# The 64-row stores of an output stage: two issuing queues, or one

## The chip, the cores and the metric

One core of one Trainium2 chip. The metric is device time in microseconds (us) of one execution; medians of several executions are quoted, and lower is better. The program runs for some 437 us; the change touches only its last 25.

## The reference, cut to what matters

Attention with a forget gate over 8 batches of 576 rows, then a mixing of the 64 lowest Fourier modes over the sequence, and a last step that adds, multiplies and clips:

```python
    X = np.fft.rfft(x, axis=1)                        # x: attention output (8, 576, 512)
    ...                                               # 64 modes times w_r, w_i
    y = np.fft.irfft(Y, n=S, axis=1)
    u = x + y
    return (u + np.maximum(u @ w_ch, 0.0)).astype(np.float32)     # (8, 576, 512), 9.44 MB
```

The kernel makes `u` and `z = u @ w_ch` as sums in PSUM, and the last line above is its output stage.

## The kernel before

Two batches form a pair. A pair's 576 rows are four blocks of 128 and a last one of 64; the two last blocks share one tile, batch b in partitions 0 to 63 and batch b+1 in partitions 64 to 127. Each "job" is one such tile. For each job PE fills `pu` and `pz`, Activation copies `pu` to SBUF (`emit_u`), VectorE adds the clipped `pz` (`emit_o`), and the result is stored. Jobs are pipelined by one: the copy for the next job is issued ahead of the sum for this one.

```python
        def emit_u(job, ps, u, split=False):
            ...
                nc.scalar.copy(u[:, bs, :], ps[0][:, bs, :])

        def emit_o(job, ps, u, o, pair, split=False):
            ...
                nc.vector.scalar_tensor_tensor(
                    o[:, bs, :], ps[1][:, bs, :], 0.0, u[:, bs, :], ALU.max, ALU.add
                )
                ...
                if sb == 4:                                   # the 64-row job of a pair
                    for h in range(2):
                        eng = (nc.sync, nc.scalar)[h]
                        eng.dma_start(
                            out[b + h, 512:576, :], o[64 * h : 64 * h + 64, 0, :]
                        )
                ...
                elif sb % 2 or n_wide < 2:                    # wide jobs: 512 KB a batch
                    ...
                        nc.sync.dma_start(...)
...
            if not last:
                uo_n = outs(jobs[n + 1])
                emit_u(jobs[n + 1], nxt, uo_n[0])
            emit_o(job, ps, *uo, n == 0)
```

There are four pairs; "the very last" half-store is the fourth pair's. In profile lines the tile of a 64-row job is `uo` (as is that of the first pair's other jobs), that of wide jobs `us` and `os`. An engine's sequencer is the part of it that issues instructions and transfers; what has been issued on a queue and not yet moved I call its ring. A **half-store** below is one of the eight stores of 64 rows, 128 KB in packets of 2,048 bytes.

The softmax here doesn't subtract the row's maximum and nothing guards it: scores larger than these inputs give would overflow.

Of the kernel before, what the change touches and what calls it, by code (L numbers as in the profile page):

```python
# [21 lines left out]
def kernel(  # L22
# [11 lines left out]
    nc = tc.nc  # L34
# [194 lines left out]
    with ExitStack() as actx:  # L229
# [486 lines left out]
        for s in range(NS + 1):  # L716
            pr, h = s // 2, s % 2
# [37 lines left out]
    with ExitStack() as bctx:  # L755
# [216 lines left out]
        def wide(job):  # L972
            return len(job) == 2 and job[0][0] != job[1][0]
# [28 lines left out]
        def emit_o(job, ps, u, o, pair, split=False):  # L1002
            for i in range(2 if split else 1):
                bs = slice(i, i + 1) if split else slice(0, len(job))
                nc.vector.scalar_tensor_tensor(  # L1005
                    o[:, bs, :], ps[1][:, bs, :], 0.0, u[:, bs, :], ALU.max, ALU.add
                )
                b, sb = job[0]
                n_wide = 4 * (b // 2 - 1) + sb
                if sb == 4:  # L1010
                    for h in range(2):
                        eng = (nc.sync, nc.scalar)[h]
                        eng.dma_start(
                            out[b + h, 512:576, :], o[64 * h : 64 * h + 64, 0, :]
                        )
                elif not wide(job):
                    nc.sync.dma_start(
                        out[b, 128 * sb : 128 * sb + 256, :].rearrange(
                            "(p r) e -> p r e", r=2
                        )[:, bs, :],  # L1020
                        o[:, bs, :],
                    )
                elif sb % 2 or n_wide < 2:
                    rs = slice(sb % 2 if n_wide < 2 else 0, sb % 2 + 1)
                    for j, (bj, _) in enumerate(job):
                        nc.sync.dma_start(
                            out[bj, 128 * (sb - sb % 2) :, :][0:256, :].rearrange(
                                "(p r) e -> p r e", r=2
                            )[:, rs, :],
                            pair[:, j, rs, :],  # L1030
                        )
# [12 lines left out]
        jobs = []  # L1044
# [42 lines left out]
        for n, job in enumerate(jobs):  # L1087
            last = n == len(jobs) - 1
            zs = terms(job, ps, 1, "xy" if n else "y")
            us = []  # L1090
            if not last:
                nxt = start(n + 1)
                us = terms(jobs[n + 1], nxt, 0, "xy")
            if n == 0:
                run(us)
                run(zs)
            elif n == 1:
                run(terms(job, ps, 1, "x"), terms(jobs[2], nxt, 0, "x"))
                run(terms(job, ps, 1, "y"))
                run(terms(jobs[2], nxt, 0, "y"))  # L1100
            elif wide(job):
                run(zs)
                run(us)
            elif len(job) == 1:
                run(us)
                run(zs)
            else:
                run(zs, us)
# [5 lines that stand above are left out]
                ps, uo = nxt, uo_n  # L1114
# [28 lines left out]
```

## Time and profile before

| | |
|---|---|
| time, median (lowest to highest) | 437.63 us (437.6 to 438.23), 3 runs |
| span of the profiled execution | 436.5 us |
| first 64-row job starts on VectorE | 410.29 us |
| last VectorE result / last store landed | 428.16 / 435.40 us |
| half-stores on Sync / on Activation | 4 / 4 |

I call the time from the first 64-row job's start on VectorE to the last landing "the stage". It has two parts: **feed**, to the last VectorE result (428.16 - 410.29 = 17.87 us), and **drain**, from there to the last landing (7.24 us). The lines of the chain, the timelines and the DMA rate are in the prediction.

### The profile page before, as it was taken

The page shows a single profiled execution, that of the slowest core. Times are in us where ns is not written, and L with a number is a line of the kernel's source. Part 1 is how long each engine was busy: PE and PEld are TensorE (multiplying, and loading weights), DVE is VectorE, ACT ScalarE, POOL GpSimd, SP SyncE. Part 2 cuts the span into 40 slices and gives each one's busy share as a digit, 9 for nine tenths or more (in the row PEclk, how much of TensorE's full clock was granted, in tenths as well). Part 3 has the DMA queues.
Part 4 walks back from the last instruction along what each step waited for, and adds up shares of the span by engine and source line. Part 5 has one row for each costly group of instructions (what it writes and reads, how often), then busy time and mean ns, then how long its engine had stood idle before and what let it go on. Part 6 is the DMA issues. An engine that isn't in the chain of part 4 may idle for free.

```text
span 436.5 us, 12293 instructions
## 1 busy us (share of the span) xinstructions
PE 357.7 (82%) x5295; PEld 243.4 (56%) x5313; DVE 263.8 (60%) x658; ACT 224.7 (51%) x340; POOL 128.9 (30%) x202
## 2 busy tenths in 40 slices
PE   3787798999797886877877886999979978899881
PEld 2454666776675665565655665766644544454440
DVE  5797888877565564665666677333233645553892
ACT  2887489775444636436447282233424434542670
POOL 7333332423233233232332232332223232200500
PEclk9996899998766857758759597799999999989997
DMA  8999999999999999999999999999999999994797
GB/s 175 236 235 237 239 235 238 235 211 237 233 215 237 226 223 237 211 237 234 214 237 211 211 212 211 211 211 212 211 212 211 211 211 211 211 211 84 273 341 276
DMA packets 50981, 97.37 MB, mean 223 GB/s; under 512 B 3792, under 2 KB 12976, under 8 KB 50928
## 3 DMA queue, kind: packets, MB, share of 16 engines
q0 software_dynamic: 46688, 86.16, 100.7%
q1 hardware_dynamic: 3920, 9.91, 6.3%
q8 instruction: 41, 0.67, 0.6%
q10 hardware_dynamic: 320, 0.52, 0.5%
q14 instruction: 12, 0.10, 0.1%
HBM read 163.73 MB, written 9.44 MB: 397 GB/s over the span
## 4 chain that ended last, share of the span: by engine, by line
DMA 40%; PE 26%; ACT 10%; DVE 7%; issue 4%; POOL 0%; DVEq 0%; ACTq 0%
DMA wb<-in_moe_w_i_dram 39%; ACT E L576 7%; PE pav L614 6%; PE ps L569 5%; PE A L188 5%; PE tp L307 4%; ACT KT L320 2%; DVE QTs L322 2%; PE vp L541 2%; DVE os L1005 1%; PE px L657 1%; PE pz L828 1%; ACT VT L326 1%; PE px L682 1%; DVE E L591 1%
## 5 line engine op out<-in xcount | busy, mean ns | idle before, releaser
L576 ACT ACTIVATE E<-ps 128x1024 bf16<-128x1024 f32 (+1 forms) x128 | 101.4, 851 | 21.7 <-PE ps L569 11.3
L188 PE MATMUL A<-XT,wb 128*128 128x16 bf16 x1984 | 70.4, 181 | 13.6 <-DMA wb<-in_moe_w_i_dram 8.9
L188 PEld LDWEIGHTS <-wb 128*128 128x128 bf16 x1984 | 63.7, 99 | 27.3 <-issue 11.4
L93 POOL DMA_DIRECT2D wb<-in_moe_w_r_dram x64 | 42.4, 663 | 119.6 <-DMA wb<-in_moe_w_r_dram 21.9
L569 PE MATMUL ps<-QTs,KT 64*128 64x64 bf16 (+4 forms) x384 | 56.8, 316 | 19.6 <-ACT E L576 17.7
L93 POOL DMA_DIRECT2D wb<-in_moe_w_i_dram x64 | 42.3, 661 | 87.3 <-DMA wb<-in_moe_w_i_dram 43.9
L614 PE MATMUL pav<-va,E 128*128 128x65 bf16 (+1 forms) x1088 | 53.1, 205 | 3.2 <-DVE x_all L636 2.6
L614 PEld LDWEIGHTS <-E 128*128 128x128 bf16 (+1 forms) x1088 | 43.5, 111 | 18.4 <-issue 9.3
L591 DVE TENSOR_TENSOR E<-E,trimask 128x256 bf16<-128x256 bf16 (+2 forms) x128 | 36.9, 302 | 20.5 <-ACT E L576 20.2
L867 ACT CAST XW<-pxw 128x512 bf16<-128x512 f32 x36 | 20.8, 587 | 39.4 <-PE pxw L860 34.5
L326 ACT COPY VT<-tp 128x640 bf16<-128x640 bf16 (+1 forms) x32 | 23.2, 761 | 32.4 <-PE tp L307 32.4
L569 PEld LDWEIGHTS <-KT 64*128 64x128 bf16 x384 | 18.8, 97 | 32.5 <-issue 20.9
L860 PE MATMUL pxw<-wch,yy 128*128 128x512 bf16 x133 | 35.1, 398 | 1.3 <-issue 0.5
L910 ACT CAST XW<-pB 128x512 bf16<-128x512 f32 x36 | 21.0, 586 | 27.8 <-PE pB L828 27.7
L320 ACT COPY KT<-tp 128x640 bf16<-128x640 bf16 (+1 forms) x32 | 21.9, 748 | 25.9 <-PE tp L307 25.8
L909 DVE CAST x_all<-pA 128x512 bf16<-128x512 f32 x36 | 24.9, 692 | 14.0 <-PE pA L828 12.4
L322 DVE COPY QTs<-tp 128x640 bf16<-128x640 bf16 (+1 forms) x32 | 23.4, 767 | 14.3 <-PE tp L307 14.0
L636 DVE TENSOR_TENSOR x_all<-pav,rcp 128x384 bf16<-128x384 f32 x64 | 29.1, 455 | 0.9
L153 DVE TENSOR_TENSOR YTe<-A,Yacc 128x128 bf16<-128x128 f32 x16 | 5.9, 367 | 33.1 <-PE A L188 33.1
L828 PEld LDWEIGHTS <-ident_bf 64*64 64x64 bf16 (+1 forms) x348 | 15.8, 108 | 17.9 <-issue 8.9
L625 DVE RECIPROCAL rcp<-pav 128x6 f32<-128x6 f32 x64 | 12.1, 189 | 20.0 <-PE pav L614 19.4
L860 PEld LDWEIGHTS <-yy 128*128 128x128 bf16 x144 | 12.7, 101 | 15.2 <-DVE yy L854 4.6
(143 smaller groups left out, 622.2 us busy)
## 6 DMA issues: line engine op xcount, KB each, us to landing
wb<-in_moe_w_r_dram POOLq DMA_DIRECT2D x62, 512.0 KB, 16.9
wb<-in_moe_w_i_dram POOLq DMA_DIRECT2D x62, 512.0 KB, 17.8
stv<-in_v_dram POOLq DMA_DIRECT2D x10, 576.0 KB, 15.1
out_dram<-os SPq DMA_DIRECT2D x10, 512.0 KB, 5.0
stk<-in_k_dram POOLq DMA_DIRECT2D x11, 288.0 KB, 15.3
stq<-in_q_dram POOLq DMA_DIRECT2D x11, 288.0 KB, 15.3
wx<-in_v_dram POOLq DMA_DIRECT2D x5, 576.0 KB, 15.5
out_dram<-uo SPq DMA_DIRECT2D x3, 512.0 KB, 4.0
```

Source lines behind the costliest of these rows:

```text
L93: keep(nc.gpsimd.dma_start(dst, src))
L188: ins = nc.tensor.matmul(A[:, eb, mi, :], lhsT=w_of(mi, eb * 128), rhs=x_of(m), start=(i == 0), stop=(i == len(terms) - 1),)
L320: nc.scalar.copy(rows(KTs[pr % 2][:, :, 0:S]), tv)
L322: ins = nc.vector.tensor_copy(rows(QT[pr][:, :, :]), tv)
L326: nc.scalar.copy(rows(VTs[pr % 2][:, :, 0:S]), tv)
L569: nc.tensor.matmul(ps[:, b, o : o + n], lhsT=KTs[pr % 2][bs, h, jb * 128 : (jb + 1) * 128], rhs=QT[pr][bs, h, jb * 128 + c0 : jb * 128 + c ...
L576: nc.scalar.activation(E[:, :, piece * 512 : piece * 512 + w], ps[:, :, 0:w], ACT.Exp, scale=scale,)
L591: nc.vector.tensor_tensor(dg, dg, tr, ALU.mult)
L614: nc.tensor.matmul(pav[64 * half : 64 * half + w, slot, :], lhsT=E[:, b, c : c + (w - 1) * st + 1 : st], rhs=va[:, jb, b, :], start=(n == ...
L636: nc.vector.tensor_tensor(xo, pi, ri, ALU.mult)
L860: nc.tensor.matmul(pxw[:, :], lhsT=xT[:, eb, i * 128 : (i + 1) * 128], rhs=wch[:, eb, :], start=(eb == 0), stop=(eb == NDC - 1),)
L909: nc.vector.tensor_copy(xs, pA[:, :])
```

## The change

Its intent: stop the Activation engine from issuing stores between its copies. Only the very last half-store, when Activation has nothing else left, stays on its queue.

```diff
-                        eng = (nc.sync, nc.scalar)[h]
+                        eng = nc.scalar if job is jobs[-1] and h else nc.sync
```

## The prediction

> **What bounds the kernel now.** I read the slices of the page first, then the DMA queues and issues, then the last 30 us in three views: the chain that ended last, the timelines of the Activation and Sync engines, and the DMA's rate in stretches of that time. The changed line runs only there.
>
> The slices (10.9 us each) show a kernel that reads weights at the DMA's pace until about 400 us; the last three slices are the output stage, with the DMA engines 70 to 90% busy and 273 to 341 GB/s moved.
>
> ```profile
> DMA  8999999999999999999999999999999999994797
> GB/s 175 236 235 237 239 235 238 235 211 237 233 215 237 226 223 237 211 237 234 214 237 211 211 212 211 211 211 212 211 212 211 211 211 211 211 211 84 273 341 276
> ```
>
> The issues (KB each, median us to landing) say how much the change touches: eight stores of 128 KB, four on each queue. Three of the four on the Activation queue move to the Sync queue, 0.39 MB of 9.44 MB written.
>
> ```profile
> out_dram<-uo SPq DMA_DIRECT2D x4, 128.0 KB, 5.6
> out_dram<-uo ACTq DMA_DIRECT2D x4, 128.0 KB, 5.2
> ```
>
> The chain of the output stage (start us, us, what) shows where an Activation issue is on the path. "ACTq L1013" is the store's issue on the Activation sequencer; here it stands between one VectorE result and the next Activation copy.
>
> ```profile
> 410.29 0.70 DVE uo L1005
> 411.00 0.02 issue
> 411.02 0.57 ACTq L1013
> 411.59 0.04 issue
> 411.63 1.02 ACT us L1000
> 412.65 0.02 issue
> 412.67 1.23 DVE os L1005
> ```
>
> It occurs once. In the second and third pair the timeline of the Activation engine has the issue in time that the engine spends waiting for PE anyway: the copy at 417.33 follows the end of the `pu` matmuls at 417.31 (chain: 416.84 + 0.47), while the issue had ended at 416.79 + 0.49 = 417.28.
>
> ```profile
> 415.58 1.02 ACT L1000 COPY us<-pu 128x1024 f32<-128x1024 f32 x1
> 416.79 0.49 ACTq L1013 DMA_DIRECT2D out_dram<-uo  x1
> 417.33 3.02 ACT L1000 COPY us<-pu 128x1024 f32<-128x1024 f32 x3 [0.73 <-PE pu L828]
> ```
>
> The DMA rate in stretches (columns: stretch, us, busy time of PE, PEld, DVE, ACT and POOL with counts, granted clock, DMA share, GB/s) is the view that decides the end:
>
> ```profile
> 416.50:417.00 0.50, 0.50 (x16) 0.35 (x12) 0.32 (x2) 0.09 (x1) 0.00 (x0) 1.00 0.10 37
> 417.00:418.50 1.50, 1.42 (x32) 0.75 (x25) 1.29 (x2) 1.17 (x2) 0.00 (x0) 1.00 1.03 401
> 418.50:421.00 2.50, 2.12 (x38) 1.28 (x32) 2.50 (x3) 1.96 (x3) 0.00 (x0) 1.00 0.97 290
> 421.00:424.00 3.00, 2.45 (x44) 1.29 (x40) 2.69 (x3) 2.28 (x4) 0.00 (x0) 1.00 1.02 411
> 424.00:426.00 2.00, 1.63 (x26) 0.84 (x28) 1.93 (x2) 1.92 (x3) 0.00 (x0) 1.00 1.00 304
> 428.00:430.00 2.00, 0.00 (x0) 0.00 (x0) 0.16 (x1) 0.00 (x0) 0.00 (x0) 1.00 1.04 420
> 430.00:434.70 4.70, 0.00 (x0) 0.00 (x0) 0.00 (x0) 0.00 (x0) 0.00 (x0) 0.71 0.79 274
> ```
>
> The DMA runs dry once, at 416.5 (37 GB/s), and from 417 to 430 its engines are about 100% busy. The last compute instruction ends at 428.16 (VectorE, 427.48 + 0.68), the last packet about 434.7, the last landing is 435.4, the span 436.5: the end is a backlog of stores. Supply and drain are nearly equal: VectorE makes a pair's 4 x 512 KB + 2 x 128 KB = 2.36 MB in 5.70 us (`uo` starts at 416.08, 421.78, 427.48), 414 GB/s; the DMA drains at 401 to 420. Yet in two stretches it moves only 290 and 304 GB/s while as busy. By the packet records these are the times when packets of the Activation queue are in flight: its 64 packets of 2,048 bytes are spread from 418.5 to 421 and from 424 to 426. There they took a mean of 134 to 222 ns per half microsecond, and the Sync queue's 4,096-byte packets 183 to 217; with the Sync queue alone the same sizes took 84 and 160 ns.
>
> **What the Trainium skill says.** "DMA: Bandwidth & Descriptors", section "Issuing engines are not separate DMA queues": stores from Sync and Activation end on the same 16 engines and interleave, and a second issuer saves only sequencer time. The trace agrees that one queue fills the engines (420 GB/s at share 1.04 with the Sync queue alone). Section "Queues, rings and completion order" of that page: an engine takes the rows that have work in turn, a packet at a time. The trace agrees as far as the 64 Activation packets lie scattered among Sync packets over 2 us. That such turns lower the rate no page states; I have it from the packet times alone. "Perfetto Trace Analysis", section "DMA Instruction — HWDGE (DVE, Sync)": an issue's span is waiting for the descriptor generator and generating, not the movement. So long Sync issues (0.53, 0.76, 1.42 and 1.76 us for the four 128 KB stores, though all are alike) are back-pressure of a full ring; the Activation issues stay at 0.47 to 0.57.
>
> **The change, part by part.** The order of instructions on PE, VectorE and POOL is the same in both kernels; Activation loses three issues, Sync gains three, each right behind its twin.
>
> (1) Removed from Activation: 3 issues of 0.57, 0.49 and 0.47, 1.53 us. On the path only the first. Without it the copy at 411.63 can start when its `pu` matmuls end, about 411.07 (the last two start at 410.50 and take 0.55); it ends at 412.10, and VectorE, which finishes its previous `os` at 412.12, goes on at 412.15 instead of 412.67. That is 0.52 us, and all later work of the stage, whose VectorE gaps are 0.2 us, moves with it; the rows of `yy` it needs have landed by 414.1, before use. The second and third give 0.03 each: 0.05 us at most.
>
> (2) Added to Sync: 3 issues. In the first pair 0.4 to 0.55 us behind 411.54, done by 412.1 when the next `os` is ready. In the second, 417.3 to about 418.1, while Sync waits until 419.1. In the third Sync would be held from about 424.1 to 425.5, with the next `os` ready at 424.8 (425.33 less 0.52): 0.7 us late. But such an issue is long because the ring is full, so the engines have work: nothing on the path.
>
> (3) DMA rate. The hole at 416.5 moves 0.5 us earlier with its store. From then on, if mixing queues is what slows the two stretches, they go at about 405 GB/s: 2.5 us x 290 = 725 KB in 1.79 us, 0.71 saved; 2.0 x 304 = 608 KB in 1.50, 0.50 saved; 1.21 in all. I count a bit over half, 0.65: the first stretch is partly a ring running empty (share 0.97, not 1.03; the next `os` comes only at 419.6), and engines that finish at different times lose rate without any mixing. The tail from 430, where the very last 128 KB still goes on Activation, keeps its 274 GB/s.
>
> Sum: 0.5 + 0.65 = 1.15 us of 437.63: 436.5.
>
> **The rivals.** (a) Only the shift counts, the slow stretches are drain and imbalance: 437.1. For it: half of a pair's 128 KB was on Sync already, and 426.5 to 427.5 is at 334 GB/s with hardly any Activation packet. (b) The whole mixing loss comes back: 435.9. For it: the packet times double just there. (c) The end is set by drain alone and the time saved ahead only lengthens the backlog; nothing changes: 437.6. Against it: the DMA ran dry at 416.5, so it has been fed late. (d) The longer Sync sequence starves the engines or delays the last `os` by the 0.7 us of part 2: 438.2. Against it: the Sync ring holds over 2 us of work when its issues take 1.4 us (issued by 431.2, drained at 434.7). (e) The compute order shifts and a buffer wait appears; the nearest reuse, a buffer stored at 417.1 (landed 422.6) and rewritten at 425.2, leaves 2.6 us.
>
> **Range and chances.** From all of the mixing loss and a little more (435.4) to nothing or the loss of (d) cut short (437.7). Two per cent is 8.75 us, over a quarter of the whole output stage; no mechanism here comes near it, so within 2% has 0.98.
>
> **What would show it.** Right: no Activation issue between 410 and 413, the second `os` of the first pair at about 412.15 rather than 412.67 (relative to the `uo` before it: 1.86 us after its start instead of 2.38); the last `uo` of VectorE 0.5 us earlier; and no stretch near 290 GB/s before the tail. If the rate in the stretches stays near 300 with one queue, the mixing step is wrong and (a) holds. If the hole at 416.5 closes or a new one opens between 419 and 426, parts 2 or 3 are wrong. If runs scatter by over 0.6 us, as the three of before do (437.6 to 438.23), the size can't be read from the medians alone.

## More of the kernel before

The wide stores have 128 partitions and most of them 512 KB in packets of 4,096 bytes.

One more answer of the rate view, for the hole and the drain (columns: stretch, us, busy time of PE, PEld, DVE, ACT and POOL with counts, granted clock, DMA share, GB/s):

```profile
416.00:417.00 1.00, 0.79 (x16) 0.57 (x19) 0.81 (x3) 0.59 (x1) 0.00 (x0) 1.00 0.43 162
...
428.16:435.40 7.24, 0.00 (x0) 0.00 (x0) 0.00 (x0) 0.00 (x0) 0.00 (x0) 0.76 0.78 286
```

In the first line the DMA has half run dry (share 0.43, 162 GB/s) while PE and VectorE work. In the last all engines are done, and 286 GB/s x 7.24 us = 2.07 MB of stores are still to move.

## The result, and the profile after

A ratio here is the mean time of one kernel's fast runs over that of the other's fast runs of the same rounds, so not quite the ratio of the medians that are quoted.

| | before | after | ratio (95% interval) |
|---|---|---|---|
| first rounds (6 and 6 runs) | 438.31 | 436.92 | 0.9968 (0.9953 to 0.9982) |
| repeated later (11 and 6 runs) | 438.10 | 437.80 | 0.9987 (0.9966 to 1.0009) |

The prediction was 436.5 us, 435.4 to 437.7, from a median of 437.63 for before. The first rounds fall inside it, and both ratios are within 2%. The repeat shows how thin the ground is: its median lies just outside the range, and its interval includes no change at all. Over both, the 12 runs of after have a mean of 437.20 us and the 17 of before 438.13, 0.93 us apart (0.84 if the 17 further runs of before are counted in, 438.03 over all 34); single runs of after scatter from 435.96 to 438.93. The repeat ran on another chip than the four experiments that came before it, so times are compared within the same rounds only.

The DMA's last three slices now carry 225, 374 and 293 GB/s; before they were 273, 341 and 276. The queues are as intended, seven half-stores on Sync and one on Activation:

```profile
out_dram<-uo SPq DMA_DIRECT2D x7, 128.0 KB, 4.7
out_dram<-uo ACTq DMA_DIRECT2D x1, 128.0 KB, 4.8
```

In the chain of the first pair, the Activation issue and the Activation copy are gone; the second `os` starts 0.01 us after PE's matmuls.

```profile
410.81 0.43 PE pu L828 x8
411.24 0.61 PE pz L828 x8
411.85 0.47 PE pu L828 x6
412.32 0.01 issue
412.33 1.24 DVE os L1005
```

And VectorE runs its four `os` without a gap, where before it idled 0.56 us ahead of the second:

```profile
411.09 4.73 DVE L1005 SCALAR_TENSOR_TENSOR os<-pz,us 128x1024 f32<-128x1024 f32 x4
```

The first `uo` now starts at 410.48, so that second `os` comes 1.85 us after it, where it was 412.67 - 410.29 = 2.38. The Activation timeline shows the reason: three copies in a row start at 411.29, 0.81 us after the `uo`, not 1.34 as in the kernel before.

```profile
411.29 3.20 ACT L1000 COPY us<-pu 128x1024 f32<-128x1024 f32 x3 [0.25 <-PE pu L828]
```

The Sync timeline (start, us for all the issues merged in a row, count) shows the other side: two half-stores hold the Sync sequencer 1.62 us in the first pair and 2.74 and 2.46 us in the next ones.

```profile
411.20 1.62 SPq L1013 DMA_DIRECT2D out_dram<-uo  x2
412.92 3.79 SPq L1026 DMA_DIRECT2D out_dram<-os  x6
416.80 2.74 SPq L1013 DMA_DIRECT2D out_dram<-uo  x2
419.63 3.25 SPq L1026 DMA_DIRECT2D out_dram<-os  x4
422.97 2.46 SPq L1013 DMA_DIRECT2D out_dram<-uo  x2
```

And the DMA rate, with the columns as above:

```profile
416.00:417.00 1.00, 1.00 (x24) 0.64 (x23) 0.81 (x2) 0.23 (x2) 0.00 (x0) 1.00 1.06 397
417.50:419.50 2.00, 1.54 (x28) 0.67 (x23) 1.79 (x3) 1.92 (x3) 0.00 (x0) 1.00 1.00 387
419.50:421.00 1.50, 1.50 (x24) 0.93 (x17) 1.50 (x2) 1.10 (x3) 0.00 (x0) 1.00 0.84 260
424.00:425.50 1.50, 1.12 (x22) 0.55 (x17) 1.50 (x2) 1.42 (x2) 0.00 (x0) 1.00 1.03 415
425.50:426.50 1.00, 0.92 (x12) 0.23 (x5) 1.00 (x2) 0.59 (x2) 0.00 (x0) 1.00 1.00 311
427.83:434.20 6.37, 0.00 (x0) 0.00 (x0) 0.00 (x0) 0.00 (x0) 0.00 (x0) 0.64 0.86 314
```

Three things are to be seen. The hole at 416.5 is closed: 397 GB/s, where the same microsecond of before had 162. There are still slow stretches, 260 and 311 GB/s, with Sync alone; in the first the engines are only 84% busy, so it also ran partly empty. And the drain is 6.37 us at 314 GB/s. Feed and drain by the two traces of each kernel:

| trace | feed | drain | stage |
|---|---|---|---|
| before, first / second | 17.87 / 17.88 | 7.24 / 7.45 | 25.11 / 25.33 |
| after, first / second | 17.35 / 17.42 | 6.37 / 6.67 | 23.72 / 24.09 |

So by the means of the traces the stage is 1.3 us shorter, 0.5 in the feed and 0.8 in the drain. The stage is a better measure than the run time, since what comes before it has nothing to do with the change and its end moves by 1.7 us from trace to trace (the first `uo` starts between 409.56 and 411.28 us in the nine traces).

### The profile page after: what moved, and what is told of

Same layout as the page of the kernel before. It is cut to its first block, busy times and chain, and to the rows that moved or that the text cites. A ratio compares the mean times of both kernels' runs of the same rounds, so it can differ in the third digit from the quotient of the medians.

```text
span 435.5 us, 12294 instructions
## 1 busy us (share of the span) xinstructions
PE 361.2 (83%) x5295; PEld 245.6 (56%) x5313; DVE 264.0 (61%) x658; ACT 224.8 (52%) x340; POOL 128.6 (30%) x202
## 3 DMA queue, kind: packets, MB, share of 16 engines
HBM read 163.73 MB, written 9.44 MB: 398 GB/s over the span
## 4 chain that ended last, share of the span: by engine, by line
PE 39%; DMA 23%; ACT 12%; DVE 10%; issue 4%; POOL 0%; DVEq 0%; ACTq 0%
DMA wb<-in_moe_w_i_dram 22%; ACT E L576 8%; PE pav L614 8%; PE A L188 7%; PE ps L569 7%; PE tp L307 5%; PE px L657 3%; DVE QTs L322 2%; PE vp L541 2%; PE pu L828 2%; ACT KT L320 2%; PE pz L828 1%; DVE XT L671 1%; DVE os L1005 1%; DVE E L591 1%
## 5 line engine op out<-in xcount | busy, mean ns | idle before, releaser
L569 PE MATMUL ps<-QTs,KT 64*128 64x64 bf16 (+4 forms) x384 | 58.2, 322 | 19.9 <-ACT E L576 17.9
L614 PE MATMUL pav<-va,E 128*128 128x65 bf16 (+1 forms) x1088 | 55.2, 209 | 3.1 <-DVE x_all L636 2.6
L614 PEld LDWEIGHTS <-E 128*128 128x128 bf16 (+1 forms) x1088 | 45.3, 114 | 18.7 <-issue 9.1
L867 ACT CAST XW<-pxw 128x512 bf16<-128x512 f32 x36 | 20.7, 586 | 35.7 <-PE pxw L860 23.5
L860 PE MATMUL pxw<-wch,yy 128*128 128x512 bf16 x133 | 33.6, 385 | 1.2 <-issue 0.7
L541 PE MATMUL vp<-ident_bf,VT 128*128 128x128 bf16 x160 | 17.1, 247 | 5.2 <-DVE QTs L322 4.6
```

The source lines that it names most:

```text
L541: nc.tensor.transpose(vp[:, sc, :, :].rearrange("p b d -> p (b d)"), VTs[s // 2 % 2][:, h, sc * 128 : (sc + 1) * 128], ident_bf[:, :],)
L569: nc.tensor.matmul(ps[:, b, o : o + n], lhsT=KTs[pr % 2][bs, h, jb * 128 : (jb + 1) * 128], rhs=QT[pr][bs, h, jb * 128 + c0 : jb * 128 + c ...
L614: nc.tensor.matmul(pav[64 * half : 64 * half + w, slot, :], lhsT=E[:, b, c : c + (w - 1) * st + 1 : st], rhs=va[:, jb, b, :], start=(n == ...
L860: nc.tensor.matmul(pxw[:, :], lhsT=xT[:, eb, i * 128 : (i + 1) * 128], rhs=wch[:, eb, :], start=(eb == 0), stop=(eb == NDC - 1),)
```

## The experiments

My theory: a path part (an Activation issue on the chain, 0.5 us) and a rate part (stores from two queues slow the DMA engines). Rivals: only the path; only the rate; and, for the rate, that half-stores are slow by themselves on whatever queue. All kernels up to the stores-only ones gave correct results. Their ratios are against the kernel before in the same rounds.

| run | ratio (95% interval) | feed | drain | stage |
|---|---|---|---|---|
| first pair only | 0.9979 (0.9965 to 0.9993) | 17.39 | 7.47 | 24.86 |
| first pair only, again | 0.9986 (0.9967 to 1.0005) | 17.40 | 6.59 | 24.00 |
| later pairs only | 0.9987 (0.9971 to 1.0002) | 17.86 | 6.82 | 24.69 |
| Activation issues deferred | 0.9995 (0.9977 to 1.0014) | 17.34 | 7.59 | 24.92 |
| all on Sync | 0.9977 (0.9964 to 0.9991) | 17.34 | 6.18 | 23.52 |
| before, again | 0.9999 (0.9983 to 1.0014) | 17.88 | 7.45 | 25.33 |

**First pair only.** The theory's path part by itself:

```diff
-                        eng = (nc.sync, nc.scalar)[h]
+                        eng = (nc.sync, nc.scalar)[h if b else 0]
```

> Only the first pair's second half-store goes to the Sync queue; those of the second and third pair stay on Activation. Theory (a path part and a rate part): VectorE's output stage, from the start of the first pair's uo to its last result, falls from 17.87 us to about 17.35, as in the changed kernel; the rate stays low while Activation packets fly in pairs two and three, so the end is only about 0.5 to 0.7 us earlier than before. Rival 'only the path': the whole 1.4 us of the changed kernel is here too (ratio 0.997). Rival 'only the rate': nothing is gained (ratio 1.000).

The feed is the changed kernel's, as every theory had it. The drain line:

```profile
426.96:434.43 7.47, 0.00 (x0) 0.00 (x0) 0.00 (x0) 0.00 (x0) 0.00 (x0) 0.64 0.77 284
```

It drains like the kernel before: 284 GB/s and 7.47 us. Of the 0.48 us gained in the feed 0.23 are given back in a longer drain. The hole at 416.5 closed here too (391 GB/s in the 1.3 us after the second `uo`). The time, 0.21% less or 0.9 us, lies between the theory's 0.5 to 0.7 and the whole 1.4, and its interval excludes neither.

**First pair only, once more**, because one trace decides little:

> First pair alone once more. If the shift of 0.52 us is mostly swallowed by the backlog of stores: stage 17.39 us and then about 7.4 us again, total 24.8, ratio 0.998 to 0.999. If it is handed on to the end: stage total 24.6 or less, with a drain of 7.2 us or less.

```profile
428.44:435.03 6.59, 0.00 (x0) 0.00 (x0) 0.00 (x0) 0.00 (x0) 0.00 (x0) 0.61 0.85 318
```

The same kernel, the same feed (17.40), and a drain 0.88 us shorter, at 318 GB/s. A single drain is therefore no proof of anything. Here the stage is 1.1 us shorter than in the first trace of before, so the shift is handed on and more. Whether it is or not changes from run to run.

**Later pairs only**, the complement:

```diff
-                        eng = (nc.sync, nc.scalar)[h]
+                        eng = nc.scalar if job[0][0] in (0, 6) and h else nc.sync
```

> The complement: the first pair's second half-store stays on Activation, those of pairs two and three go to Sync. Theory: VectorE's stage stays at 17.87 us; from its last result to the last landing 7.24 us falls to about 6.4, the end is 0.7 to 0.9 us earlier (ratio 0.998). Rival 'only the path': no gain (1.000). Rival 'only the rate': all 1.4 us (0.997).

```profile
427.90:434.72 6.82, 0.00 (x0) 0.00 (x0) 0.00 (x0) 0.00 (x0) 0.00 (x0) 0.56 0.87 314
```

No shift in the feed (17.86), and the drain is at 314 GB/s and 6.82 us: a stage 0.42 us shorter than in the first trace of before. The hole stays (216 GB/s in 415.82 to 417.12). The theory had the drain at about 6.4 us, so it gave half of what was expected. That speaks against "only the path" but doesn't rule it out: 0.42 us is less than the 0.88 by which the two drains of the first-pair kernel differ, and the ratio, 0.9987, is by itself not clear of 1.

**Deferred.** All queues as before, but the Activation issue is pinned three jobs later, behind the fourth `us` copy, where Activation idles:

```diff
-                        eng = (nc.sync, nc.scalar)[h]
-                        eng.dma_start(out[b + h, 512:576, :], o[64 * h : 64 * h + 64, 0, :])
+                        args = (out[b + h, 512:576, :], o[64 * h : 64 * h + 64, 0, :])
+                        if h == 0:
+                            nc.sync.dma_start(*args)
+                        elif job is jobs[-1]:
+                            nc.scalar.dma_start(*args)
+                        else:
+                            pending.append([3, args])
...                                                  # after emit_u of the next job
+                for x in pending:
+                    x[0] -= 1
+                while pending and pending[0][0] == 0:
+                    keep(nc.scalar.dma_start(*pending.pop(0)[1]))
```

> All queues as in the kernel before, but the Activation issue of each pair comes three jobs later, behind the fourth us copy, where Activation has 0.4 to 0.6 us idle. So the hold on the path is gone and the mixing of queues is not. Theory: VectorE's stage 17.35 to 17.45 us, end 0.5 us earlier than before, with rates of 290 to 340 GB/s while the Activation packets fly. Rival 'only the path': 1.4 us earlier, as the changed kernel. Rival 'mixing is all': no gain.

```profile
428.62:436.21 7.59, 0.00 (x0) 0.00 (x0) 0.00 (x1) 0.00 (x0) 0.00 (x0) 0.59 0.76 282
```

Here the two parts are separated in one kernel: the whole shift (17.34) and, with the Activation stores kept, the slow drain (282 GB/s). The stage is 0.2 us shorter than that of the first trace of before, and the ratio 0.9995. This suggests that taking the issue off the path is worth less than its 0.5 us while the stores go on two queues, since the stage ends with the stores and a feed that is earlier lengthens their queue. It is not shown: the interval (0.9977 to 1.0014) includes the full 0.5 us (0.9989).

**All on Sync**, the last half-store too:

```diff
+                        eng = nc.sync
```

> The very last half-store too on Sync. Theory: the changed kernel moves 238 to 352 GB/s from 3.4 to 4.4 us after the last VectorE result, when the last Activation packets fly; with Sync alone that stretch runs at about 400 and the end is 0.2 to 0.4 us earlier than the changed kernel's, unless the last issue, which waits for the ring at 1.2 to 1.4 us a piece, comes too late: then it is up to 0.5 us later. Rival 'mixing costs nothing': the same or later, by the length of the last issue.

The stage is 23.52 us, 0.2 less than the first trace of after and 0.6 less than the second; the ratio 0.9977 can't be told from after's 0.9968 and 0.9987. The drain rate is 317 GB/s, after's 314. The slow stretch of the drain went on, only later: 340 GB/s from 3.4 to 4.4 us after the last VectorE result, where about 400 was expected, and 260 from 4.0 to 5.0. So no effect of the last half-store's queue on the drain's rate is seen in this one trace, and this version is not shown to be better.

**The stores by themselves.** Five kernels: no compute but copies on Activation that space its issues, and the whole 9.44 MB stored from one tile with no wait for data. Their outputs are wrong, which doesn't matter for the times. Their core:

```python
    for b in range(0, 8, 2):
        for c in range(5):
            keep(nc.scalar.copy(dst[:, :], src[:, :]))        # about 1 us each
        ...                                                   # four 512 KB stores, on Sync
        for h in range(2):
            eng = nc.scalar if h in H_ON_ACT else nc.sync     # H_ON_ACT: (), (1,) or (0, 1)
            keep(eng.dma_start(out[b + h, 512:576, :], o[64 * h : 64 * h + 64, 0, 0, :]))
```

All half-stores on Sync:

> Wrong result on purpose: only the stores of the output stage, 16 of 512 KB and 8 of 128 KB, all issued on Sync from one tile with no wait for compute, while Activation makes copies. It measures the disputed rate by itself. Every theory: 9.44 MB at about 405 GB/s, some 23.5 us from the first packet to the last. If half-stores slow the engines by themselves, on whatever queue, it is nearer 350 GB/s and 27 us.

One of each pair on Activation:

> Wrong result on purpose: the same stores, with one half-store of each pair on Activation, some 5 us apart. Mixing theory: 0.3 to 0.5 us lost for each of the four, so 1.2 to 2 us longer than with Sync alone, and rates of about 300 GB/s while they fly. Rival 'mixing costs nothing, the slow stretches came from running empty': within 0.2 us of Sync alone.

Both on Activation:

> Wrong result on purpose: the suspected cost doubled, both half-stores of each pair on Activation. Mixing theory: twice the loss of one half, 2.4 to 4 us longer than Sync alone. Rival: within 0.2 us.

Half-stores on Sync, one 512 KB store of each pair on Activation (`n > 3` in the loop that is cut above):

> Wrong result on purpose: one 512 KB store of each pair on Activation, with 4,096-byte packets over all 128 partitions, and both half-stores on Sync. If any two queues together slow the engines, it loses as much or more than one half-store (1.2 us or more); if it is the small packets or the 64 partitions of a half-store beside wide ones, it loses little (under 0.5 us).

And all on Sync, but each 128 KB read from all 128 partitions:

```diff
-                    out[b + h, 512:576, :], o[64 * h : 64 * h + 64, 0, 0, :]
+                    out[b + h, 512:576, :].rearrange("p (r e) -> (p r) e", r=2),
+                    o[:, h, 0, 0:256],
```

> Wrong result on purpose: the stores by themselves, all on Sync, but each half-store of 128 KB read from all 128 partitions in packets of 1,024 bytes instead of from 64 partitions in packets of 2,048. The rate with Sync alone fell to 221 to 320 GB/s for about a microsecond at each pair of half-stores, some 0.35 us a pair. If it is the 64 partitions, those dips go and the span falls from 31.2 us to about 30. If it is the small packets, they stay or grow: 31.2 us or more.

| stores only | span | against all on Sync |
|---|---|---|
| all on Sync | 31.2 us | |
| one half-store a pair on Activation (4) | 31.7 us | +0.5, 0.13 each |
| both half-stores on Activation (8) | 32.3 us | +1.1, 0.14 each |
| one 512 KB store a pair on Activation (4) | 31.3 us | +0.1, 0.03 each |
| all on Sync, 128 partitions | 30.0 us | -1.2, 0.15 for each of 8 |

(One run each, so of unknown state, and the last one on another chip than the four above it; the granted clock was 1.0 in all five.) By the span a half-store on Activation costs 0.13 us more than on Sync, and twice as many cost twice as much: a rate part shows, but a quarter to under a half of the 0.3 to 0.5 us that I expected. The even 0.13 is partly luck: by the packet records, up to the last 0.1 MB the loss is 0.71 us for four and 0.92 for eight, 0.18 and 0.12 each, and the spans also hold the time of that last 0.1 MB, which goes from 0.96 to 1.34 us among these three. All on Sync, first packet to last took 25.1 us, between the 23.5 and the 27 that were expected. It isn't a matter of two queues as such, since a wide store on Activation costs 0.03. What I had not separated is larger: a half-store is slow on any queue. With Sync alone, the stretch around a pair of half-stores is the middle line here (columns: stretch, us, busy time of DVE, ACT and POOL with counts, clock, DMA share, GB/s):

```profile
6.00:9.90 3.90, 0.00 (x0) 3.77 (x5) 0.00 (x0) 1.00 1.02 406
9.90:11.00 1.10, 0.00 (x0) 1.07 (x2) 0.00 (x0) 1.00 0.96 276
11.00:15.50 4.50, 0.00 (x0) 4.37 (x5) 0.00 (x0) 1.00 1.04 417
```

The same bytes from 128 partitions, although in packets half as large:

```profile
6.00:9.90 3.90, 0.00 (x0) 3.77 (x5) 0.00 (x0) 1.00 1.03 406
9.90:11.00 1.10, 0.00 (x0) 1.07 (x2) 0.00 (x0) 1.00 0.98 354
11.00:15.50 4.50, 0.00 (x0) 4.37 (x5) 0.00 (x0) 1.00 1.02 405
```

276 GB/s become 354 while the wide stores before it run at 406 in both. (Of the 1.2 us, 0.5 lie in the last 0.1 MB, where the half-stores come last: it took 1.14 us from 64 partitions and 0.68 from 128.) The engines are 96 to 98% busy in both: busy is not fast. The Trainium skill has a page that I did not consult for the prediction and that fits: "SBUF — State Buffer", section "Door 1: The DMA port swizzle (why `[64,N]` ≈ `[32,N]`)" says that the rate depends on how many of 16 ports the partitions reach, and that partitions 0 to 63 reach the eight even ones and 64 to 127 the eight odd ones. The runs agree in direction; no record here shows a port, so the mechanism is the page's and not shown by these runs. "DMA: Bandwidth & Descriptors", section "Rules for kernel authors", says of two transfers to disjoint partition halves to use one of 128 partitions instead. The run with 128 partitions kept two transfers and widened each, so its 1.2 us point the same way without testing that advice.

**The two kernels again**, with five rounds, for their scatter:

> The kernel before once more, unchanged: shows how far two traces and two sets of runs of the same kernel differ. Ratio 1.000. Output stage: 17.87 us from the first pair's uo to VectorE's last result, as every theory has it; then 7.0 to 7.5 us to the last landing if the 7.24 of the first trace is the rule, and near 6.4 if the long drain was chance.

```profile
428.01:435.46 7.45, 0.00 (x0) 0.00 (x0) 0.00 (x1) 0.00 (x0) 0.00 (x0) 0.73 0.78 291
```

> The changed kernel once more, with five rounds. Ratio near 0.997; stage 17.35 us, then 6.2 to 6.5 us to the last landing if the shorter drain belongs to the change, near 7.2 if it was chance. The runs of one store pattern by itself put the loss by an Activation half-store at 0.13 us, so three of them explain 0.4 us of the drain, not 0.86; a drain of 6.7 to 6.9 here would fit that.

```profile
428.14:434.81 6.67, 0.00 (x0) 0.00 (x0) 0.00 (x0) 0.00 (x0) 0.00 (x0) 0.61 0.87 313
```

291 GB/s and 313: each kernel's second drain runs at nearly the rate of its first (286 and 314). Sorted by where the second halves of the second and third pairs go (the same queue for both in every kernel), the nine drains are 7.24, 7.45, 7.47, 6.59 and 7.59 us on Activation and 6.37, 6.67, 6.82 and 6.18 on Sync: means of 7.27 and 6.51, with one of the nine out of order. The 0.76 us between the means is more than the 0.26 us that two such stores cost by themselves.

Cutting each drain 5 us after the last VectorE result shows where most of it lies. Before, then after:

```profile
428.16:433.16 5.00, 0.00 (x0) 0.00 (x0) 0.00 (x0) 0.00 (x0) 0.00 (x0) 0.88 1.02 373
433.16:435.40 2.24, 0.00 (x0) 0.00 (x0) 0.00 (x0) 0.00 (x0) 0.00 (x0) 0.50 0.25 91
```

```profile
427.83:432.83 5.00, 0.00 (x0) 0.00 (x0) 0.00 (x0) 0.00 (x0) 0.00 (x0) 0.68 1.02 372
432.83:434.20 1.37, 0.00 (x0) 0.00 (x0) 0.00 (x0) 0.00 (x0) 0.00 (x0) 0.50 0.28 106
```

For 5 us both kernels drain at the same rate; in all nine traces it is 362 to 381 GB/s, and the second group is no faster (a mean of 370 against 376). What differs is the end, in which on the mean only a quarter of the 16 engines is busy (share 0.25 and 0.28). By the packet records the last 0.1 MB takes a mean of 1.60 us in the first group and 1.09 in the second, which is 0.51 of the 0.76 us; the one drain out of order has a short end too (1.17). The 286 and 314 GB/s are thus not two speeds of moving, but mostly the same speed with a longer or a shorter end. Why the end is longer when those half-stores go on Activation, the runs do not settle.

## Why the prediction was right, and where it was not

**The end is a backlog of stores, not compute.** Right: the changed feed is 0.5 us shorter in every kernel that moves or defers the first pair's issue, but the time is not shown to follow it in full.

**Step 1, the Activation issue on the path, 0.52 us, once.** Right in size and place: the feed went from 17.87 and 17.88 to 17.35 and 17.42 us, and the second `os` to 1.85 and 1.93 us after the `uo` (1.86 predicted). Moving only the later pairs' stores left it at 17.86, so the second and third issue were indeed off the path.

**Step 2, what Sync takes on.** Right as far as the traces go that nothing of it lengthened the stage, wrong in the first pair. "0.4 to 0.55 us" for the added issue were 1.04 us (1.20 in the second trace of after, though 0.59 in the kernel with all on Sync), and the first `os` store, whose data was ready at 412.30, was issued at 412.92, 0.6 us late. And "the hole at 416.5 moves 0.5 us earlier" was wrong: it closed, in both traces of after (397 and 381 GB/s in 416 to 417), which the prediction itself had named as a sign that part 2 or 3 is wrong. It closed in every kernel with the earlier feed, the deferred one too (share 1.02), and stayed in the kernel that changes only the later pairs; the likely reason is that the first pair's bytes move later and the next `os` comes earlier. In the third pair the added issue ended at 425.43 and the next store waited about 0.5 us for it (0.7 predicted), with the rate at 415 GB/s up to 425.5: the ring did have work. That long Sync issues mean a full ring is inferred, since no view shows a ring. The stores-only run fits: with no data to wait for, the first two issues of 512 KB took 0.38 and 0.42 us, and two of 128 KB behind four of 512 KB 1.23 and 1.28, the time in which 512 KB move at 426 and 410 GB/s.

**Step 3, the rate, 0.65 us.** The sum came out near (0.8 us by the traces), but by another way than the step had it; that it did is luck. Two of its claims failed. First, "no stretch near 290 GB/s before the tail": 260 and 311 remain with Sync alone. By the prediction's own sign mixing is then not what makes the stretches slow, and rival (a) is nearer, which put them down to drain and imbalance; the stores-only runs name a cause that no rival of the prediction had, that half-stores slow the engines by themselves. Second, "the tail from 430 keeps its 274 GB/s": the gain appeared mostly there, with a drain at 313 and 314 GB/s against 286 and 291, although the last half-store is on Activation in both kernels, and mostly in its last 0.1 MB. The 1.21 us of loss by mixing, from which I took a bit over half, was mis-sized: the two stretches hold one Activation half-store each, which at 0.13 us are 0.26 us by the stores-only runs, 0.4 with the first pair's. I had read packet times of 134 to 222 ns beside Activation packets as the price of mixing; part of that is the price of the half-stores. (Smaller slips of reading: the ranges of packet times leave out half microseconds with means down to 112 and 171 ns, and the last packet ended at 435.07, not 434.7.)

**The sum.** 0.5 + 0.65 = 1.15 us was predicted; 0.32% and 0.13% less time came out in the two sets of rounds, 1.4 and 0.6 us of 438, and 1.3 by the stage in the traces. With the measured terms, 0.5 for the path and 0.4 for the mixing, the estimate is 0.9, near what the runs together show (0.84 to 0.93). Since the path part may not be fully handed on, as the deferred kernel suggests, and most of the drain's gain lies in its end, that agreement is not a proof of the split.

**Open.** Why a half-store is dearer on the second queue; why the end of the drain, in which few engines still work, differs between kernels and, in the first-pair kernel, between two traces (1.74 and 1.17 us for the last 0.1 MB); and how much of the path's 0.5 us reaches the run time. The obvious next kernel was not tried: to lay the 64-row jobs out so that each batch's 64 rows fill 128 partitions, as in the stores-only run with 128 partitions, which needs other matrices on PE. One store for both halves needs care too: "DMA: Bandwidth & Descriptors", section "Why a DMA increments its semaphore by 16 and not by 1", says that the number of engines must divide the slowest dimension of both sides, and a destination of two batches has 2 there; no run here shows it.

## What to carry to other kernels

Where an output stage ends in a backlog of stores, ask of a saved wait how much of it the DMA's queue will swallow: here 0.5 us off the compute chain went with 0.2 us at the end in one trace and 1.1 in another of the same kernel. DMA engines that are 96% busy are not at their rate: look at GB/s beside the share, and at which stores are in flight when the two part; a stretch with stores from 64 partitions ran at 276 GB/s in a stream of 406. Where the end of a drain is compared, look apart at the last stretch in which the share falls: a mean rate over both hides which of them changed. And when the effect is a third of a per cent, measure the stage in several traces and the suspect by itself, because neither one trace nor six runs settle it.

## What the Trainium skill lacked or had wrong

- "DMA: Bandwidth & Descriptors", "Issuing engines are not separate DMA queues", says that a second issuer only saves the sequencer's issue time. In the stores-only runs a 64-partition store on the second queue cost 0.13 us more of the span than on the first (31.7 against 31.2 us for four, 32.3 for eight), a 128-partition store of 512 KB 0.03 us (one run each).
- The same section calls the issue time usually small relative to the DMA itself. With a backlog ahead it was not: in the kernel before, one 128 KB store held the Sync sequencer 1.76 of the 6.0 us to its landing, with 0.31 us of data at the 420 GB/s that the engines moved just before; an issue of such a store with little ahead of it held it 0.53 us.
- "SBUF — State Buffer", "Door 1: The DMA port swizzle", explains half the ports for 64 partitions, and the page gives rates for such a transfer alone and for two halves at once, but no cost for such a store among wide ones: 0.15 us for each 128 KB (31.2 against 30.0 us for eight), and 276 against 354 GB/s around a pair of them.
- No page has the price, for the stores behind it, of an issue that waits on a full ring: in the changed kernel a store whose data was ready at 412.30 was issued at 412.92.
